# Four attention layers on one core: the order of all work written out as a literal, 274 exponentials on VectorE in place of 182

## The chip, the core and the metric

The kernel runs on one core of a Trainium2 chip. A core has five engines, each with its own instruction stream: TensorE (PE in the profile, its weight loads PEld), VectorE (DVE), ScalarE (ACT), GpSimd (POOL) and SyncE (SP), which here only issues DMAs. An engine takes its instructions in the order in which the program lists them; semaphores hold an instruction until what it needs is there. The metric is the device time of one execution in microseconds.

## The reference

Four transformer attention layers run one after the other over 2048 tokens of width 512, with weights A, B, A, B. All 32 heads share one key and one value head of width 16.

```python
q = (x @ wq).reshape(B, S, H, Dh).transpose(0, 2, 1, 3)     # H = 32, Dh = 16
k = x @ wk
v = x @ wv
scores = einsum("bhqd,bkd->bhqk", q, k) * Dh ** -0.5
p = softmax(scores)
o = einsum("bhqk,bkd->bhqd", p, v)
return o.transpose(0, 2, 1, 3).reshape(B, S, H * Dh) @ wo

x = x + A(layernorm(x));  x = x + B(layernorm(x))
x = x + A(layernorm(x));  x = x + B(layernorm(x))
```

The exponentials are the bulk of it: 4 layers x 32 heads x 2048 x 2048 of them.

## The kernel before, in words

**Tiling.** Queries are cut into 4 blocks `b` of 512, heads into 4 groups `m` of 8, keys into 16 chunks `c` of 128. A *pair* is one (layer, block, group); there are 64. A pair is worked in two halves of four heads (`odd`), and each half is a *segment*, cut further in the first pairs of each layer, whose last keys do not exist yet. There are 156 segments. A *unit* is one key chunk of one segment; there are 2048. No maximum is subtracted before the exponential; a check of the ranges at the end (`verdict`) sends the program to a second, general path if the inputs are too large, which does not run here.

**Scores.** `scores(n)` (L630 to L667) takes half a unit: two matmuls write 128 keys x 512 queries each of two heads into one PSUM tile `st` of 128 x 1024. Three such tiles exist (`NST = 3`), so TensorE can be three ahead of whoever reads them. Each of the 4096 halves is then read by one exponential.

**Exponentials.** Most are one ScalarE instruction (L660), written into a ring `pt` of 8 tiles. In a unit of the set `split` the first half goes to VectorE instead (`v_exp`, L669 to L690): a TENSOR_SCALAR (L673) reads `st` and writes an integer `e`, and six more instructions (L684, L686, L687, L688, L689, L679) turn it into the exponential with a cubic, in a tile `dpt`. The other half of the same unit goes through ScalarE into the same `dpt`. There are two `dpt` tiles, one `e` and one `mant`. The first read of `st` frees it; the other six run from SBUF.

**Weighted values.** `pv(u)` (L692 to L715) multiplies the exponentials of a whole unit with the values: four float32 matmuls (each is two records in the trace) in four column strips of the array, summed over the units of a segment into an accumulator `acc`. At a segment's end `merge` (L565 to L628) has VectorE read `acc` into `num` and `den` (two instructions, L575 or L578). After the second segment of a pair, five more instructions divide (L599 to L603, led by a RECIPROCAL) and give `ot`.

**Background work.** Everything else is made of generators that yield between pieces: queries (L434), keys and values (L391), layer norm and transposes (L349), output projections (L477), weight loads (L297). A piece is mostly three float16 matmuls that stand for one product of higher precision. A sum over several pieces is *open* from its first piece to its last. PSUM has eight banks: six are the three `st` tiles, two are called `acc0` and `acc1`. One of the two holds the running segment's sum, the other is used by the background work.

**What sets the order.** The program lists every instruction by a planner that runs while the program is built. It keeps a clock of TensorE, VectorE and ScalarE with fixed costs (L55 to L62) and, at each step, lets a short beam search (`choose`, L65 to L118, ten steps deep) say whether half a unit of scores (S), a unit of weighted values (P) or a piece of background (M) is next. VectorE's side work waits in a list `bg.low` and is let out one instruction at a time when the clock says that VectorE is free (L748). A half goes to VectorE only under the rule below; `GAP = 8` units must lie between two, and none is taken in the last six units of a segment.

```python
split_next = (nxt % 2 == 0 and n and not bg.low and clk.dve <= now + 600        # L761
              and segs[n[0]][3] - n[1] >= TAIL and nxt // 2 - state["split"] >= GAP
              and clk.exp >= now + BEHIND and ("v", l, NB - 1) in bg.done)
```

When the first P of a new segment is due, the planner finishes an open background sum first and gives the new segment the other bank:

```python
if s not in acc:                                                                # L697
    bg.close()
    clk.pe = max(clk.pe, bg.bank)
    state["idle"] = 1 - s % 2
    acc[s] = aps.tile([P, 512], F32, name="acc", tag=f"acc{s % 2}")
```

Of the kernel before, what the change touches and what calls it, by code (L numbers as in the profile page):

```python
# [19 lines left out]
P = 128  # L20
# [37 lines left out]
T_V1, T_V2, T_V3 = 1250, 750, 1250  # L58
GAP, TAIL, BEHIND = 8, 6, 0

DEPTH, WIDTH = 10, 24
P_S, P_P, P_M, P_URGENT, ACT = 266, 1000, 800, 1600, 4.0  # L62


def choose(root, price, bank):  # L65

    beam = [(0, root, 0, "")]
    for _ in range(DEPTH):
        new = {}
        for _, state, worth, work in beam:
            now, mode, exp, free, done, half, dve, room, units, is_open, steps, m_at, m_ns = state
            if room:
                at = max(now, free[0]) + CHANGE.get(mode + "S", 0) + T_S
                w = worth + P_S
                if dve:
                    e = exp  # L80
                    end = max(dve, at + LATE) + T_V1 + SYNC
                    whole = end + 2 * T_V2 + 4 * T_V3
                    lag = max(e, at + LEAD - T_S + CHANGE["MS"] - T_EXP)
                else:
                    e = lag = max(exp + T_EXP, at - T_S + LEAD)
                    end = whole = e + SYNC
                    w += ACT * T_EXP
                if not half:
                    d = done
                elif half > whole:  # L90
                    d = tuple(sorted(done + (half,)))
                else:
                    d = done + (whole,)
                n = (at, "S", e, free[1:] + (end,), d, 0 if half else whole, 0, room - 1, units, is_open,
                     steps, m_at, m_ns)
                c = at + ACT * lag - w
                if n not in new or c < new[n][0]:
                    new[n] = (c, n, w, work or "S")
            if done and (units or not is_open):
                at = max(now, done[0], 0 if units else bank) + CHANGE.get(mode + "P", 0) + T_P  # L100
                u = units - 1 if units else 99
                n = (at, "P", exp, free, done[1:], half, dve, room + 2, u, is_open, steps,
                     m_at if u else max(m_at, at + LATE + 1250 + SYNC), m_ns)
                w = worth + P_P
                c = at + ACT * max(exp, max(at, free[0]) + CHANGE["PS"] + LEAD - T_EXP) - w
                if n not in new or c < new[n][0]:
                    new[n] = (c, n, w, work or "P")
            if steps and (is_open or units >= (steps + 1) // 2):
                at = max(now, m_at) + CHANGE.get(mode + "M", 0) + m_ns
                n = (at, "M", exp, free, done, half, dve, room, units, steps > 1, steps - 1, m_at, m_ns)  # L110
                w = worth + m_ns - 3 * T_MM + price
                c = at + ACT * max(exp, max(at, free[0]) + CHANGE["MS"] + LEAD - T_EXP) - w
                if n not in new or c < new[n][0]:
                    new[n] = (c, n, w, work or "M")
        if not new:
            break
        beam = sorted(new.values(), key=lambda n: n[0])[:WIDTH]
    return beam[0][3]  # L118


class Clock:


    def __init__(self):
        self.pe = 0
        self.dve = 0
        self.mode = "M"
        self.exp = -T_EXP

    def change(self, mode):  # L130
        return CHANGE.get(self.mode + mode, 0)

    def mm(self, ns, mode="M"):
        self.pe += self.change(mode) + ns
        self.mode = mode

    def act(self):

        self.exp = max(self.exp + T_EXP, self.pe - T_S + LEAD)
        return self.exp + SYNC  # L140

    def v(self, ns):
        self.dve = max(self.dve, self.pe + LATE) + ns


class Background:
# [3 lines left out]

    def __init__(self, clk):
        self.clk = clk
        self.first = deque()
        self.low = deque()
        self.later = deque()
        self.queue = self.first
        self.done = set()
        self.open = False
        self.ready = self.bank = 0
        self.steps, self.ns = 0, 0  # L160
# [7 lines left out]
    def left(self):  # L168
        return self.first or self.later

    def at(self):
        return self.ready if self.open else max(self.ready, self.bank)

    def step(self):
        while self.left():
            if not self.open:
                self.queue = self.first or self.later
            if self.steps:
                self.clk.pe = max(self.clk.pe, self.at())
            self.steps -= 1  # L180
            try:
                self.open, self.ready, *more = next(self.queue[0])
                if not self.open:
                    self.steps, self.ns = more or (0, 0)
                return True
            except StopIteration:
                self.queue.popleft()
                self.open, self.ready, self.steps = False, self.clk.dve + SYNC, 0
                return True
        return False  # L190

    def others(self):

        while self.left() and not self.steps and self.ready <= self.clk.pe:
            self.step()

    def close(self):
        while self.open:
            self.step()

    def need(self, key):
        while key not in self.done:
            assert self.step() or self.spare(), key

    def spare(self):

        if self.low:
            ns, op = self.low.popleft()
            op()
            self.clk.dve = max(self.clk.dve, self.clk.pe) + ns  # L210
            return True
        return False
# [3 lines left out]
def fast_path(ctx, tc, x_in, weights, out, flag):  # L216
# [4 lines left out]
    xts = ctx.enter_context(tc.tile_pool(name="xts", bufs=6))  # L221
# [6 lines left out]
    ends = []  # L228
    scr = ctx.enter_context(tc.tile_pool(name="scr", bufs=1, space=DRAM))

    clk = Clock()
    bg = Background(clk)
    state = dict(idle=0, pool=None, end=False, split=-GAP, merged=0)
# [63 lines left out]
    def load_split(key, w):  # L297
# [3 lines left out]
        for c in range(NC + 2):  # L301
            if c > 1:
                t = ts[c - 2]
                V.tensor_scalar(parts[0][:, c - 2], t, WS, None, ALU.mult)
                V.scalar_tensor_tensor(parts[1][:, c - 2], t, WS, parts[0][:, c - 2],
                                       ALU.mult, ALU.subtract)
                clk.v(1100)
# [3 lines left out]
            if c:  # L311
                yield False, clk.pe + 4000
# [252 lines left out]
    def merge(s):  # L565
# [60 lines left out]
        if n < BQ:  # L626
            while bg.spare():
                pass  # L628
# [318 lines left out]
```

## Time and profile before

| what | value |
|---|---|
| time, median of 3 runs | 3728.27 us (3727.08 to 3729.49) |
| the profiled execution's own time | 3728.57 us |
| its span, first to last instruction | 3726.8 us |
| granted TensorE clock, mean | 0.995 |
| TensorE busy | 3640.9 us (98%) |
| ScalarE busy | 3613.7 us (97%), 3914 exponentials |
| VectorE busy | 2403.0 us (64%), 182 exponentials of seven instructions |
| GpSimd busy | 108.2 us (3%) |
| DMA | mean 29 GB/s |

Two engines are nearly full over the whole span and a third at two thirds. Busy time of TensorE is the time covered by matmuls from their start to a modelled end, so a matmul that is followed late can hide a short wait; how far apart matmuls start says more. ScalarE's exponentials overlap: one lasts 1076 ns by its row, and 3732 of them cover 3460.4 us, or 927 ns each.

### The profile page before, as it was taken

How to read it: one execution, taken by the hardware profiler on the slowest of the kernel's cores; microseconds unless marked ns; L12 is line 12 of the kernel's file. 1: busy time of each engine (PE TensorE's matmuls, PEld its weight loads, DVE VectorE, ACT ScalarE, POOL GpSimd, SP SyncE). 2: the span in 40 equal slices, each digit the busy share in tenths (PEclk: the TensorE clock that was granted, in tenths of full speed). 3: DMA queues.
4: the chain of work that ended last, by engine and by line, in shares of the span. 5: the costliest groups of instructions: out<-in, count | busy, mean ns of one | idle time of the engine just before them, and what ended most of it. 6: DMA issues, size and time to landing. Idle time of an engine off the chain costs nothing. (4 is left out here: it accounts for less than half of the span.)

```text
span 3726.8 us, 62299 instructions
## 1 busy us (share of the span) xinstructions
PE 3640.9 (98%) x26707; PEld 894.4 (24%) x26707; DVE 2403.0 (64%) x2962; ACT 3613.7 (97%) x3920; POOL 108.2 (3%) x122
## 2 busy tenths in 40 slices
PE   7899999999999999999999999999999999999998
PEld 2222222222222222222222222222222222222221
DVE  4576667567656766767655666666765566666665
ACT  6899999999999999999999999999999999999997
POOL 1000000000000000000000000000000000000000
PEclk9999999999999999999999999999999999999999
DMA  2110000110010000000101010000101101000000
GB/s 87 46 43 26 27 18 18 32 35 29 27 43 18 26 21 27 29 24 27 29 32 43 13 37 14 31 21 15 46 15 41 35 21 34 18 30 28 23 19 13
DMA packets 94814, 108.07 MB, mean 29 GB/s; under 512 B 15936, under 2 KB 72256, under 8 KB 94528
## 3 DMA queue, kind: packets, MB, share of 16 engines
q1 hardware_dynamic: 94208, 102.95, 8.7%
q8 instruction: 211, 3.46, 0.4%
q0 software_dynamic: 320, 1.05, 0.1%
q14 instruction: 75, 0.61, 0.1%
HBM read 70.39 MB, written 33.55 MB: 28 GB/s over the span
## 5 line engine op out<-in xcount | busy, mean ns | idle before, releaser
L660 ACT ACTIVATE pt<-st 128x1024 f32<-128x1024 f32 x3732 | 3460.4, 1076 | 67.1 <-PE st L645 66.0
L707 PE MATMUL acc<-pt,vop 128*32 128x512 f32 x14928 | 1920.1, 603 | 6.1 <-DVE qs L451 3.9
L645 PE MATMUL st<-qt,kop 64*128 64x512 f16 x8192 | 1316.5, 382 | 48.5 <-ACT pt L660 17.7
L645 PEld LDWEIGHTS <-kop 64*128 64x128 f16 x8192 | 348.2, 94 | 1727.6 <-issue 1654.2
L673 DVE TENSOR_SCALAR e<-st 128x1024 int32<-128x1024 f32 x182 | 222.9, 1225 | 775.6 <-PE st L645 775.4
L707 PEld LDWEIGHTS acc<-pt,vop 128*32 128x32 f32 x14928 | 340.8, 108 | 701.6 <-issue 670.4
L689 DVE SCALAR_TENSOR_TENSOR dpt<-dpt,mant 128x1024 f32<-128x1024 f32 x182 | 224.1, 1231 | 5.0
L679 DVE SCALAR_TENSOR_TENSOR dpt<-dpt,e 128x1024 f32<-128x1024 f32 x182 | 223.4, 1228 | 5.1
L688 DVE SCALAR_TENSOR_TENSOR dpt<-dpt,mant 128x1024 f32<-128x1024 f32 x182 | 224.1, 1232 | 3.4
L687 DVE SCALAR_TENSOR_TENSOR dpt<-mant 128x1024 f32<-128x1024 f32 x182 | 222.0, 1220 | 0.0
L599 DVE RECIPROCAL den<-den 128x512 f32<-128x512 f32 (+1 forms) x76 | 215.9, 2841 | 0.3
L660 ACT ACTIVATE dpt<-st 128x1024 f32<-128x1024 f32 x182 | 192.1, 1055 | 4.1 <-ACT pt L660 3.7
L707 PE MATMUL acc<-dpt,vop 128*32 128x512 f32 x1456 | 192.5, 601 | 0.0
L491 DVE SCALAR_TENSOR_TENSOR xt<-ops,xt 128x512 f32<-128x512 f32 x140 | 96.2, 687 | 146.0 <-PE ops L336 144.9
L684 DVE TENSOR_SCALAR mant<-e 128x1024 int32<-128x1024 int32 x182 | 129.0, 709 | 4.5
L686 DVE TENSOR_SCALAR e<-e 128x1024 int32<-128x1024 int32 x182 | 127.4, 700 | 5.3
L455 POOL TENSOR_TENSOR sq<-qs 128x512 bf16<-128x512 f16 x64 | 66.7, 1042 | 2119.1 <-DVE qs L450 2119.1
L578 DVE SCALAR_TENSOR_TENSOR num<-acc,half,num 128x512 f32<-128x512 f32 x92 | 68.9, 749 | 86.9 <-PE acc L707 86.6
L334 PE MATMUL qps<-xnT,wq 128*128 128x512 f16 x256 | 99.6, 389 | 0.7 <-ACT xnT L330 0.7
L335 PE MATMUL qps<-xnT,wq 128*128 128x512 f16 x256 | 98.0, 383 | 0.2 <-DVE xnT L384 0.2
L450 DVE TENSOR_SCALAR qs<-qps 128x512 f16<-128x512 f32 x64 | 43.9, 687 | 83.5 <-PE qps L336 72.7
L334 PE MATMUL ops<-wo,ot 128*128 128x512 f16 x252 | 97.6, 387 | 0.0
(99 smaller groups left out, 1413.3 us busy)
## 6 DMA issues: line engine op xcount, KB each, us to landing
qt<-qs SPq DMA_DIRECT2D x624, 64.0 KB, 2.2
qs<-qs SPq DMA_DIRECT2D x64, 256.0 KB, 2.2
xs<-xt SPq DMA_DIRECT2D x48, 256.0 KB, 2.0
xt<-xs SPq DMA_DIRECT2D x48, 256.0 KB, 3.2
xt<-in_A_x_dram SPq DMA_DIRECT2D x32, 256.0 KB, 3.4
out_dram<-xt SPq DMA_DIRECT2D x16, 256.0 KB, 2.0
wst<-in_A_wo_dram SPq DMA_DIRECT2D x8, 256.0 KB, 2.8
wst<-in_B_wq_dram SPq DMA_DIRECT2D x8, 256.0 KB, 2.8
```

What stands on the lines that cost most here:

```text
L334: PE.matmul(ps, a[0], b[0], start=first, stop=False)
L599: (6 * n, lambda c=c: V.reciprocal(den[:, c], den[:, c])),
L645: PE.matmul(st[:, k * 512:(k + 1) * 512], kop[l % 2][c // 4][r, (c % 4) * P:(c % 4 + 1) * P], qt[pr][r, 2 * half + odd], start=True, stop= ...
L660: e = nc.scalar.activation(pt, st, AF.Exp, scale=SCALE / UP / UP).ins
L673: V.tensor_scalar(e, st, SCALE / UP / UP * LOG2E * 2.0 ** 23, 127 * 2.0 ** 23, ALU.mult, ALU.add)
L679: V.scalar_tensor_tensor(p, p, C0, e.bitcast(F32), ALU.add, ALU.mult)
L684: (T_V2, lambda: V.tensor_scalar(mant.bitcast(I32), e, 0x7FFFFF, 0x3F800000, ALU.bitwise_and, ALU.bitwise_or)),
L686: (T_V2, lambda: V.tensor_scalar(e, e, 0x7F800000, None, ALU.bitwise_and)),
L687: (T_V3, lambda: V.scalar_tensor_tensor(p, mant, C3, mant, ALU.add, ALU.mult)),
L688: (T_V3, lambda: V.scalar_tensor_tensor(p, p, C2, mant, ALU.add, ALU.mult)),
L689: (T_V3, lambda: V.scalar_tensor_tensor(p, p, C1, mant, ALU.add, ALU.mult)),
L707: PE.matmul(acc[s][32 * j:32 * j + 32, :], v[l % 2][c // 4][:, c % 4, 16 * odd:16 * odd + 32], p_of[u, j % 2][:, (j // 2) * 512:(j // 2 + ...
```

## The change: what it does

The planner, its clock and its cost table are gone. In their place stands a string `ORDER` of 8972 letters that is walked once while the program is built. `S` is half a unit of scores with its exponential on ScalarE, `V` the same with the exponential on VectorE; `v` is the next of the six instructions that follow on VectorE; `P` and `Q` are the first or second waiting unit of weighted values; `M` and `m` are a piece of background, `l` one from the list of less urgent ones; `d` is the next instruction of a division. The string has 3822 S, 274 V, 1644 v, 2048 P and Q, 804 pieces of background and 380 d.

The instructions themselves keep their form and shape. Beside the order, these things differ:

- 92 more halves go to VectorE, and as many fewer to ScalarE.
- A background sum may stay open when a new segment begins. Then the new segment's accumulator takes the bank of the segment that has just ended, which `merge` must have read by then.
- `xts`, the pool of rows of `x`, has 8 buffers, not 6.

```diff
-T_MM, T_S, T_P, T_TR, T_EXP, LEAD, SYNC, LATE = 216, 226, 860, 490, 917, 1449, 55, 270
-CHANGE = {"SP": 89, "PS": 139, "SM": 97, "PM": 149, "MS": 96, "MP": 93}
...
-def choose(root, price, bank):
...
+ORDER = (
+    "mSSSMMMSSSPPSSMSSPPSSMMSSSPPSSMMSSPSSPPSSSPPSSMMSSSMMSPSSPSSMPSmSPSSPPSSSPmPSMSSPSSPPSSSMPSPSSSPMSSPSSPM"
+    "SSPSmSMMSSPSMMSSPSSPSSMPSmSPPSSSPPSSPmSSPMSSPSSMSPSSPPSMSSSPPSSSPMSSPSmSMMMSSSMPSSPSSPPSMSSPmSSPPSSSPPmS"
...
-    xts = ctx.enter_context(tc.tile_pool(name="xts", bufs=6))
+    xts = ctx.enter_context(tc.tile_pool(name="xts", bufs=8))
...
-    def scores(n):
+    def scores(n, on_v):
...
+        if on_v:
+            split.add(u)
...
+        if half:
+            waiting.append(u)
+        if on_v:
+            v_exp(pt, st)
             return
...
-    def pv(u):
+    def pv(k):
+
+        u = [u for u in waiting if u[0] == state["seg"]][k]
+        waiting.remove(u)
...
         if s not in acc:
-            bg.close()
-            clk.pe = max(clk.pe, bg.bank)
-            bg.bank = state["merged"]
-            state["idle"] = 1 - s % 2
-            acc[s] = aps.tile([P, 512], F32, name="acc", tag=f"acc{s % 2}")
+
+            if not bg.open:
+                state["idle"] = 1 - state["idle"]
+            acc[s] = aps.tile([P, 512], F32, name="acc", tag=f"acc{1 - state['idle']}")
             left[s] = c1 - c0
...
+        nxt = 0
+        for what in ORDER:
+            if what in "SV":
+                scores(nxt, what == "V")
+                nxt += 1
+            elif what in "PQRT":
+                pv("PQRT".index(what))
+            elif what in "Mml":
+                bg.step(what == "l")
             else:
...
+                (exp_ops if what == "v" else div_ops).popleft()()
+        assert nxt == 2 * len(units) and not waiting and not div_ops
```

How the instructions move is seen best on VectorE. Below is VectorE's list in the kernel before, from the end of the 75th segment (in layer 1), whose `acc` it reads into `num` and `den`; `e<-st` is the first instruction of a VectorE exponential, `dpt<-dpt,e` its last, and the numbers behind names count allocations.

```order
L575 TENSOR_SCALAR num_14447<-acc,half 128x512
L575 TENSOR_SCALAR den_14448<-acc,half 128x512
L688 SCALAR_TENSOR_TENSOR dpt<-dpt,mant 128x1024
L689 SCALAR_TENSOR_TENSOR dpt<-dpt,mant 128x1024
L679 SCALAR_TENSOR_TENSOR dpt<-dpt,e_14393 128x1024
L673 TENSOR_SCALAR e_14514<-st 128x1024
L684 TENSOR_SCALAR mant<-e_14514 128x1024
L686 TENSOR_SCALAR e_14514<-e_14514 128x1024
L687 SCALAR_TENSOR_TENSOR dpt<-mant 128x1024
L450 TENSOR_SCALAR qs<-qps 128x512
L451 TENSOR_TENSOR qs<-qps,qs 128x512
```

The change has this at the same place:

```order
L515 TENSOR_SCALAR num_14761<-acc,half 128x512
L515 TENSOR_SCALAR den_14762<-acc,half 128x512
L611 TENSOR_SCALAR mant<-e_14750 128x1024
L613 TENSOR_SCALAR e_14750<-e_14750 128x1024
L614 SCALAR_TENSOR_TENSOR dpt<-mant 128x1024
L615 SCALAR_TENSOR_TENSOR dpt<-dpt,mant 128x1024
L436 SCALAR_TENSOR_TENSOR xt<-ops,xt 128x512
L616 SCALAR_TENSOR_TENSOR dpt<-dpt,mant 128x1024
L617 SCALAR_TENSOR_TENSOR dpt<-dpt,e_14750 128x1024
L609 TENSOR_SCALAR e_14844<-st 128x1024
```

From this segment's end to the end of the second segment after it, the list before starts three exponentials and the list of the change four. Over the whole program two starts lie 16 halves apart at the least before, and mostly 10 to 16 halves apart in the change.

On TensorE, the kernel before has this where the 75th segment gives way to the 76th; `vop_3` and `vop_0` tell the two apart, since the first is multiplied with the last chunks' values and the second with the first ones':

```order
L645 MATMUL st<-qt,kop_0_101 128x512
L707 MATMUL acc<-pt,vop_3_112 32x512 x4
L707 MATMUL acc<-pt,vop_0_109 32x512 x4
L645 LDWEIGHTS kop_1_102
L645 MATMUL st<-qt,kop_1_102 128x512
```

The change has this there:

```order
L636 MATMUL acc<-dpt,vop_3_112 32x512
L581 LDWEIGHTS kop_0_101
...
L297 LDWEIGHTS ot_0_13556
L297 MATMUL ops<-wo_9598,ot_0_13556 128x512
L298 LDWEIGHTS ot_0_13556
L298 MATMUL ops<-wo_9599,ot_0_13556 128x512
L299 LDWEIGHTS ot_1_13557
L299 MATMUL ops<-wo_9598,ot_1_13557 128x512
L581 LDWEIGHTS kop_1_102
...
L636 MATMUL acc<-pt,vop_0_109 32x512 x8
```

Two halves of scores, the first piece of an output projection (`ops`, left open) and two more halves have come between the segments, and two units of weighted values now follow each other. Since the sum of `ops` stays open in the other bank, the 76th segment's sum goes where the 75th's was. That happens at 33 of the 155 segments' starts after the first.

More of the change, by code (lines that the diff above doesn't have):

```diff
@@ L51 @@
 LOG2E = 1.4426950408889634
-T_MM, T_S, T_P, T_TR, T_EXP, LEAD, SYNC, LATE = 216, 226, 860, 490, 917, 1449, 55, 270
-CHANGE = {"SP": 89, "PS": 139, "SM": 97, "PM": 149, "MS": 96, "MP": 93}
[L58 to L62, printed above, removed]
-def choose(root, price, bank):
[L71 to L118, printed above, removed]
@@ L121 @@
-class Clock:
-    def __init__(self):
[L125 to L143, printed above, removed]
@@ L153, in __init__ @@
+class Background:
+    def __init__(self):
         self.first = deque()
-        self.low = deque()
         self.later = deque()
@@ L166, in add_later, with step @@
         self.later.extend(gens)
[L168 to L199, printed above, removed]
-    def need(self, key):
[L202 to L212, printed above, removed]
+    def step(self, later=False):
+        if not self.begun:
+            self.queue = self.later if later or not self.first else self.first
+        self.begun = True
+        try:
+            self.open = next(self.queue[0])
+        except StopIteration:
+            self.queue.popleft()
+            self.open = self.begun = False
+    def need(self, key):
+        assert key in self.done, key
 @with_exitstack
@@ L227, in fast_path @@
     exps = []
-    ends = []
     scr = ctx.enter_context(tc.tile_pool(name="scr", bufs=1, space=DRAM))
-    clk = Clock()
-    bg = Background(clk)
-    state = dict(idle=0, pool=None, end=False, split=-GAP, merged=0)
+    bg = Background()
+    state = dict(idle=0, pool=None, end=False, seg=0)
+    exp_ops = deque()
+    div_ops = deque()
     def bank(name):
@@ L515, in verdict @@
     def verdict():
-        yield False, clk.pe, 1, T_MM
+        yield False
         n, nv = NL * NB, NL * NB + 8
@@ L560, in fast_path @@
     left = {}
-    ring = {}
-    done = {}
+    waiting = []
     split = set()
@@ L623, in then @@
                         bg.add_later(load_split(("wq", l + 2), weights[l % 2][0]))
-        bg.low.append((0, then))
-        if n < BQ:
-            while bg.spare():
-                pass
-    def scores(n):
+        op = div_ops.pop()
+        div_ops.append(lambda: (op(), then()))
+    def scores(n, on_v):
         u, half = units[n // 2], n % 2
@@ L654, in scores @@
             pt = pts[:, len(exps) % NPT]
-            ring.setdefault(u, len(exps))
         p_of[u, half] = pt
-        if u in split and half == 0:
-            v_exp(u, pt, st)
+        if half:
+            waiting.append(u)
+        if on_v:
+            v_exp(pt, st)
             return
@@ L665, in scores, with v_exp @@
             exps.append(e)
-        ends.append(clk.act())
-        done[u] = max(done.get(u, 0), ends[-1])
-    def v_exp(u, p, st):
+    def v_exp(p, st):
         e = one.tile([P, W * 512], I32, name="e2")
@@ L788, in fast_path @@
-        while bg.spare():
-            pass
+        nxt = 0
[7 more added lines that the diff above has]
+                bg.step(what == "l")
+            else:
+                (exp_ops if what == "v" else div_ops).popleft()()
+        assert nxt == 2 * len(units) and not waiting and not div_ops
         state["end"] = True
-        while bg.step():
-            pass
+        while bg.first or bg.later:
+            bg.step()
```

230 lines of the change are left out of this document (118 added, 112 removed).

## The prediction, made blind

> **What bounds the kernel now.** I read the page's busy times first, then the groups of instructions, then stretches of time, then who waits for whom, and last TensorE's timeline.
>
> ```profile
> span 3726.8 us, 62299 instructions
> PE 3640.9 (98%) x26707; PEld 894.4 (24%) x26707; DVE 2403.0 (64%) x2962; ACT 3613.7 (97%) x3920; POOL 108.2 (3%) x122
> L660 ACT ACTIVATE pt<-st 128x1024 f32<-128x1024 f32 x3732 | 3460.4, 1076 | 67.1 <-PE st L645 66.0
> L660 ACT ACTIVATE dpt<-st 128x1024 f32<-128x1024 f32 x182 | 192.1, 1055 | 4.1 <-ACT pt L660 3.7
> L707 PE MATMUL acc<-dpt,vop 128*32 128x512 f32 x1456 | 192.5, 601 | 0.0
> ```
>
> TensorE and ScalarE are both full, and the profiled execution took 3728.57 us, 0.3 above the median of the runs. The stretches show that this is so all the way, not as an average of two kinds of stage:
>
> ```profile
> 900.00:1800.00 900.00, 893.71 (x6598) 220.13 (x6591) 598.46 (x725) 890.62 (x967) 24.86 (x23) 1.00 0.09 28
> 1800.00:2700.00 900.00, 891.86 (x6581) 217.97 (x6579) 576.28 (x694) 890.83 (x968) 23.93 (x23) 1.00 0.08 27
> ```
>
> Columns: the stretch, then TensorE, weight loads, VectorE, ScalarE and GpSimd with their counts. ScalarE does 967 instructions in 890.62 us, 0.921 us each, and idles 9.4 of 900 us. Relieving it alone helps only as far as TensorE has room, so the question is how much of TensorE's 98% is work. Its timeline in the middle:
>
> ```profile
> 1499.71 1.07 PE L707 MATMUL acc<-pt,vop 128*32 128x512 f32 x8
> 1500.70 0.61 PE L645 MATMUL st<-qt,kop 64*128 64x512 f16 x4
> 1501.25 1.92 PE L707 MATMUL acc<-pt,vop 128*32 128x512 f32 x16
> 1503.11 0.61 PE L645 MATMUL st<-qt,kop 64*128 64x512 f16 x4
> 1503.64 1.06 PE L707 MATMUL acc<-pt,vop 128*32 128x512 f32 x8
> 1504.64 0.61 PE L645 MATMUL st<-qt,kop 64*128 64x512 f16 x4
> 1505.18 0.39 PE L334 MATMUL ops<-wo,ot 128*128 128x512 f16 x1
> 1505.40 0.38 PE L335 MATMUL ops<-wo,ot 128*128 128x512 f16 x1
> ...
> 1506.27 0.38 PE L336 MATMUL ops<-wo,ot 128*128 128x512 f16 x1
> 1506.58 0.61 PE L645 MATMUL st<-qt,kop 64*128 64x512 f16 x4
> ...
> 1509.64 0.39 PE L645 MATMUL st<-qt,kop 64*128 64x512 f16 x2
> 1509.96 1.07 PE L707 MATMUL acc<-pt,vop 128*32 128x512 f32 x8
> ```
>
> I read the distances from start to start. A half of scores (x2) before a P takes 0.32 us (1509.64 to 1509.96). Two halves before a P take 0.55 (1500.70 to 1501.25), so a half before a half takes 0.23. A P (x8) before scores takes 0.99 (1499.71 to 1500.70), two take 1.86 (1501.25 to 1503.11), so a P before a P takes 0.87. A background matmul takes 0.22 before its like and 0.31 before scores (1506.27 to 1506.58), and a half before background 0.54 - 0.23 = 0.31. So each change of kind has a price: S to P 0.09, P to S 0.12, M to S 0.09, S to M 0.08. For the rare M to P and P to M, which are not in this piece, I take 0.09 and 0.12 as for the same kind left or entered.
>
> With these, TensorE's floor. The built order before has 4096 halves, 2048 P and 2131 background matmuls, and of changes 1481 S to P, 1540 P to S, 398 M to S, 457 S to M, 102 M to P and 43 P to M. Work: 4096 x 0.23 + 2048 x 0.87 + 2131 x 0.22 = 942 + 1782 + 469 = 3193 us. Changes: 133 + 185 + 36 + 37 + 9 + 5 = 405 us. The floor is 3598 us. The first score starts late and the program ends long after the last P:
>
> ```profile
> 33.69 0.58 PE L645 MATMUL st<-qt,kop 64*128 64x512 f16 x1 [7.29 <-DMA qt<-qs]
> 3701.32 0.70 PE L645 MATMUL st<-qt,kop 64*128 64x512 f16 x4
> 3704.34 2.95 PE L707 MATMUL acc<-pt,vop 128*32 128x512 f32 x24
> ```
>
> From 33.7 to 3726.8 are 3693 us, some 95 to 105 over the floor, and about 18 of them lie behind the last P (3707 to 3726.8, with little matmul in it). The row at 3701.32 shows what the rest looks like: two halves that cover 0.70 us, not the 0.61 seen above. A wait of under 0.2 us hides inside TensorE's busy time, because a matmul's modelled end is later than the next one's earliest start. The waits that do show:
>
> ```profile
> PE st L645 <- ACT pt L660: 17.7, 48, 0.5
> PE st L645 <- DVE kop L415: 5.5, 3, 2.6
> PE st L334 <- DVE ot L602: 5.4, 3, 3.4
> PE acc L707 <- DVE qs L451: 3.9, 4, 1.6
> ACT pt L660 <- PE st L645: 66.0, 59, 10.6
> ```
>
> Columns: who waits for whom, total us, times, longest. So of the 100 us, 18 are the tail, some 12 to 15 are waits for VectorE and DMA, and up to 70 are waits for a free `st` tile, that is for ScalarE: 17.7 visible, the rest hidden. ScalarE in turn has 66 us of waits for TensorE, 10.6 of them at the start. Two engines of equal load (ScalarE 3914 x 0.921 = 3605 us, TensorE 3598) lean on each other through three buffers, and both lose.
>
> **The change part by part.**
>
> *Fewer changes of kind on TensorE.* The order of the change has the same matmuls, with 1401 S to P, 1388 P to S, 446 M to S, 433 S to M, 25 M to P and 38 P to M: 290 changes fewer. -80 x 0.09 - 152 x 0.12 + 48 x 0.09 - 24 x 0.08 - 77 x 0.09 - 5 x 0.12 = -7.2 - 18.2 + 4.3 - 1.9 - 6.9 - 0.6 = **-30 us**, all on the path, since TensorE bounds. The new floor is 3568 us.
>
> *92 halves from ScalarE to VectorE.* At 3460.4 / 3732 = 0.927 us this takes 85 us from ScalarE: 3822 x 0.921 = 3520 us are left, 48 under TensorE's new floor where the two were level. It shortens the path only through the waits for `st`. At most it takes all 70 us; nothing, if these come from the latency of a buffer's round and not from ScalarE's pace. I take **-40**, a little over half: 48 us of lead in 3568 is 1.3%, some 0.01 us per half, so a backlog drains only slowly.
>
> *What that costs VectorE.* The seven instructions of an exponential:
>
> ```profile
> L673 DVE TENSOR_SCALAR e<-st 128x1024 int32<-128x1024 f32 x182 | 222.9, 1225 | 775.6 <-PE st L645 775.4
> L684 DVE TENSOR_SCALAR mant<-e 128x1024 int32<-128x1024 int32 x182 | 129.0, 709 | 4.5
> L686 DVE TENSOR_SCALAR e<-e 128x1024 int32<-128x1024 int32 x182 | 127.4, 700 | 5.3
> L687 DVE SCALAR_TENSOR_TENSOR dpt<-mant 128x1024 f32<-128x1024 f32 x182 | 222.0, 1220 | 0.0
> L679 DVE SCALAR_TENSOR_TENSOR dpt<-dpt,e 128x1024 f32<-128x1024 f32 x182 | 223.4, 1228 | 5.1
> L578 DVE SCALAR_TENSOR_TENSOR num<-acc,half,num 128x512 f32<-128x512 f32 x92 | 68.9, 749 | 86.9 <-PE acc L707 86.6
> ```
>
> With L688 and L689 of the same form as L679, one is 1.225 + 0.709 + 0.700 + 1.220 + 3 x 1.228 = 7.54 us, and 92 are 694 us. VectorE goes from 2403 to 3097 us, 85% of some 3660. It hides beside TensorE and ScalarE as long as each chain ends before its P is due. Laid end to end with the distances above, TensorE has a median of 12.3 us of work between a VectorE half and its P (13.8 before), and VectorE lists 9.6 us from the chain's first to its last instruction, others in between included (9.6 before). The room is 3.4 us in the median and 1.2 us at the tenth part of the chains (4.2 and 2.1 before). Start, handing over and any backlog come out of that. For the tight tenth, 27 chains, up to 1 us each could show: 0 to +27 us. Today no P waits for a chain (0.0 before the `dpt` matmuls, above).
>
> *Sums left open over a segment's end.* At 33 starts the new sum waits until VectorE has read the old one: 2 x 0.749 = 1.5 us. Between the old sum's last P and the new one's first, the order lists at least two halves, three background matmuls and two halves: 0.23 + 0.31 + 2 x 0.22 + 0.31 + 0.23 + 0.32 = 1.84 us behind the last P's 0.99, or 1.96 behind the 0.87 that a P lasts; half of the places have 2.6 or more. So nothing shows, unless VectorE is busy with one more instruction of 1.23 us: then the 13 places with 1.96 wait 0.8 us each and some others 0.1, 0 to +12 us. For both VectorE terms I take **+5**, near the low end, since the row nearest to them is the 0.0.
>
> *At nothing:* the two further `xts` buffers (no row of the waits names the loads of `x`), and the same DMAs in another order (the queues are used 9%). The start and the 18 us tail stay.
>
> Sum: 3728.6 - 30 - 40 + 5 = **3663 us**, 1.7% less.
>
> [...]
>
> **The rivals.**
>
> *ScalarE alone is the bound.* TensorE's stretched distances would close up as soon as ScalarE is faster, and all 85 us come through: 3728.6 - 85 = 3643. For it: ScalarE's 9 us idle in 900. Against it: the piece of timeline above, in which TensorE has no gap. [...]
>
> *The waits for `st` stay.* They come from the round of three buffers (matmul, handing over, exponential, handing back) and not from ScalarE's load. Then only the changes of kind count: 3728.6 - 30 = 3699. For it: the 48 visible waits are at most 0.5 us long, so no backlog stands behind them.
>
> *VectorE late, the slower side.* VectorE works strictly in its listed order. An instruction at its head that waits for TensorE holds the rest of a chain behind it, and the P waits for that. Today it stands idle ahead of its exponentials for 775.4 us in 182 chains, and has 3727 - 2403 = 1324 us idle in all; then it has some 566. Each 0.1 us by which a chain is late on average costs 27 us; the saving of 70 us is gone at 0.26 us per chain. With 0.4 us it is 3728.6 - 70 + 110 = 3769. Against it: 3.4 us of room in the median. [...]
>
> *It hardly does what it says.* The order moves 92 halves and 290 changes, so no effect could only come from gains and losses that cancel: 3728.
>
> **How the numbers follow.** The forecast has 0.50, ScalarE alone 0.20, the waits that stay 0.17, VectorE late 0.09, no effect 0.04. Differences under 0.2% cannot be told from none in this kernel. Faster is the sum of the first three, 0.87; same 0.04; slower 0.09. The best case, all of the 70 and no loss, is 3728.6 - 100 = 3629; the range's other end takes in the rival with 3699 and 13 us of its VectorE terms: 3628 to 3712.
>
> **What would show it.** ScalarE's exponentials at x3548 and x274 and its idle time up by some 20 us, with waits for TensorE ahead of them; TensorE's wait for `pt` under 17.7 us; distances unchanged at 0.23, 0.87 and 0.99; VectorE at about 3097 us. The forecast fails if the `dpt` matmuls or the first `acc` of a segment show tens of us of idle time (VectorE late), if the changes of kind cost otherwise than by one piece of timeline, or if TensorE's floor was no floor: a span under 3602, the new floor of 3568 and the start of 34.

## The result

The change takes 3644.07 us (median of 4 runs, 3641.05 to 3644.58) where the kernel before takes 3728.3: a ratio of 0.9772, 95% interval 0.9755 to 0.9789, or 84 us less. The forecast was 3663, with 3628 to 3712 as its range. The profiled execution took 3641.05 us, its span is 3639.3 us. One of the four executions of a later run, the one with 273 VectorE halves, took 11958.87 us at a granted TensorE clock of 0.28; what is said of that run is from the other three.

Below are the profile page's and the stretches' lines of the kernel after, with the same columns as the lines of before.

```profile
span 3639.3 us, 63025 instructions
PE 3575.5 (98%) x26707; PEld 925.5 (25%) x26707; DVE 3084.4 (85%) x3606; ACT 3552.5 (98%) x3828; POOL 116.8 (3%) x122
L598 ACT ACTIVATE pt<-st 128x1024 f32<-128x1024 f32 x3548 | 3311.5, 1046 | 41.0 <-PE st L581 30.4
L636 PE MATMUL acc<-dpt,vop 128*32 128x512 f32 x2192 | 290.8, 602 | 0.0
L609 DVE TENSOR_SCALAR e<-st 128x1024 int32<-128x1024 f32 x274 | 335.3, 1224 | 199.3 <-PE st L581 194.8
...
900.00:1800.00 900.00, 896.97 (x6742) 233.61 (x6738) 762.96 (x881) 893.70 (x964) 29.52 (x25) 1.00 0.09 28
1800.00:2700.00 900.00, 896.59 (x6739) 234.78 (x6735) 764.59 (x886) 892.84 (x962) 29.58 (x25) 1.00 0.09 29
```

VectorE does 274 exponentials and is busy for 3084 us, as worked out (3097). No P waits for a VectorE chain: 0.0 ahead of the `dpt` matmuls. In the same 900 us TensorE now runs 6742 matmuls instead of 6598, 2.2% more, and its idle time there falls from 6.3 to 3.0 us. ScalarE does not idle more, as I had expected, but less: 3639 - 3553 = 87 us in all instead of 113.

The waits of the kernel after:

```profile
PE st L581 <- ACT pt L598: 8.1, 28, 0.5
PE st L581 <- DVE kop L369: 5.9, 4, 2.6
PE st L297 <- DVE ot L540: 4.7, 3, 3.4
PE st L581 <- DVE e L609: 0.5, 1, 0.5
...
ACT pt L598 <- PE st L581: 30.4, 42, 11.2
```

TensorE's visible wait for ScalarE fell from 17.7 to 8.1 us, ScalarE's for TensorE from 66.0 to 30.4. Both sides wait less. The waits that hide in busy time are seen in the distances from start to start, taken here from all matmuls of both traces by what stands ahead and what behind (S a half of scores, P a unit of weighted values, M a background matmul); "beyond" is the sum of what each distance lies over the usual one of its class.

```
            before                         after
        count  usual ns  beyond us     count  usual ns  beyond us
S to S   2158    227      114.8         2262    227       67.4
S to P   1481    319        6.3         1401    310        8.9
P to S   1540    998        3.8         1388    998        4.3
P to P    465    882        2.0          622    883        0.0
S to M    457    312        3.6          433    312        7.9
M to S    398    312       12.6          446    312       12.6
all 9    8274              167.8        8274             120.2
sum of all distances: 3705.6 us before, 3618.6 us after
```

The 87 us between the two sums are 30 for other counts at the usual distances, 47 for shorter waits between two halves of scores, and 10 spread thinly over the rest. (Ahead of a P the usual distance shrank by 9 ns, but the mean by under 3, which is 4 us.)

The traces also say who keeps a half waiting. A half needs the tile of the half three before it, and nearly every half that starts late (over 0.02 us beyond its usual distance) starts 0.04 to 0.06 us after the read of that tile has ended. Put to these readers, the late halves are ScalarE's: 106.8 us (649 halves) before and 63.8 us (516) in the change. VectorE's reads hold 4.6 us before and 0.5 us in the change. So far this is the forecast's picture, waits for tiles that ScalarE has not yet read, with the term larger. Whether the lighter ScalarE or the new order brings the 47 is for the experiments to say.

### The profile page after: what moved, and what is told of

The parts are those of the page before. It is cut to its first block, busy times and chain, and to the rows that moved or that the text cites. A ratio compares the mean times of both kernels' runs of the same rounds, so it can differ in the third digit from the quotient of the medians.

```text
span 3639.3 us, 63025 instructions
## 1 busy us (share of the span) xinstructions
PE 3575.5 (98%) x26707; PEld 925.5 (25%) x26707; DVE 3084.4 (85%) x3606; ACT 3552.5 (98%) x3828; POOL 116.8 (3%) x122
## 4 chain that ended last, share of the span: by engine, by line
PE 86%; ACT 11%; DVE 2%; DMA 1%; issue 0%; SPq 0%; POOL 0%; ACTq 0%; DVEq 0%; POOLq 0%
PE acc L636 47%; PE st L581 27%; ACT pt L598 10%; PE qps L297 2%; PE ops L297 2%; PE qps L298 1%; PE qps L299 1%; PE ops L299 1%; PE ops L298 1%; ACT dpt L598 1%; PE tps L338 1%; PE kps L297 0%; DVE den L537 0%; PE kps L299 0%; PE kps L298 0%
## 5 line engine op out<-in xcount | busy, mean ns | idle before, releaser
L598 ACT ACTIVATE pt<-st 128x1024 f32<-128x1024 f32 x3548 | 3311.5, 1046 | 41.0 <-PE st L581 30.4
L636 PE MATMUL acc<-pt,vop 128*32 128x512 f32 x14192 | 1799.5, 601 | 0.1
L609 DVE TENSOR_SCALAR e<-st 128x1024 int32<-128x1024 f32 x274 | 335.3, 1224 | 199.3 <-PE st L581 194.8
L617 DVE SCALAR_TENSOR_TENSOR dpt<-dpt,e 128x1024 f32<-128x1024 f32 x274 | 339.7, 1240 | 8.5
L615 DVE SCALAR_TENSOR_TENSOR dpt<-dpt,mant 128x1024 f32<-128x1024 f32 x274 | 338.9, 1237 | 7.1
L616 DVE SCALAR_TENSOR_TENSOR dpt<-dpt,mant 128x1024 f32<-128x1024 f32 x274 | 336.9, 1230 | 7.6
L614 DVE SCALAR_TENSOR_TENSOR dpt<-mant 128x1024 f32<-128x1024 f32 x274 | 336.4, 1228 | 0.0
L636 PE MATMUL acc<-dpt,vop 128*32 128x512 f32 x2192 | 290.8, 602 | 0.0
L598 ACT ACTIVATE dpt<-st 128x1024 f32<-128x1024 f32 x274 | 282.9, 1033 | 5.0 <-ACT pt L598 4.3
L613 DVE TENSOR_SCALAR e<-e 128x1024 int32<-128x1024 int32 x274 | 193.6, 707 | 7.9
L297 PE MATMUL qps<-xnT,wq 128*128 128x512 f16 x256 | 99.1, 387 | 1.4 <-DVE wq L269 0.7
L298 PE MATMUL qps<-xnT,wq 128*128 128x512 f16 x256 | 97.4, 380 | 0.6 <-DVE xnT L342 0.6
L299 PE MATMUL qps<-xnT,wq 128*128 128x512 f16 x256 | 97.3, 380 | 0.4 <-DVE wq L270 0.4
```

Of the source, the lines that this page charges most:

```text
L297: PE.matmul(ps, a[0], b[0], start=first, stop=False)
L598: e = nc.scalar.activation(pt, st, AF.Exp, scale=SCALE / UP / UP).ins
L609: V.tensor_scalar(e, st, SCALE / UP / UP * LOG2E * 2.0 ** 23, 127 * 2.0 ** 23, ALU.mult, ALU.add)
L613: lambda: V.tensor_scalar(e, e, 0x7F800000, None, ALU.bitwise_and),
L614: lambda: V.scalar_tensor_tensor(p, mant, C3, mant, ALU.add, ALU.mult),
L615: lambda: V.scalar_tensor_tensor(p, p, C2, mant, ALU.add, ALU.mult),
```

## The experiments

Three theories went into them. A, the forecast: TensorE's work and its changes of kind are the floor, and ScalarE adds waits for a free `st` tile. B: ScalarE alone is the bound, and the time follows its load. C: VectorE's lateness limits (first as the fixed round of the three tiles, C, then as C', the chains themselves).

### ScalarE's load halved, in both orders

```diff
-        e = nc.scalar.activation(pt, st, AF.Exp, scale=SCALE / UP / UP).ins
+        if u in split:
+            e = nc.scalar.activation(pt, st, AF.Exp, scale=SCALE / UP / UP).ins
+        else:
+            e = nc.scalar.activation(pt[:, :512], st[:, :512], AF.Exp, scale=SCALE / UP / UP).ins
...
+    V.memset(pts[:, :, 512:], 1.0)
     with tc.manual_schedule():
```

On the order of the change:

> The changed kernel, in which each ScalarE exponential of a unit that lies on ScalarE alone covers 512 of the 1024 columns; the other 512 columns of the ring are set to one at the start, so half of these exponentials are not computed. The order is untouched. It takes ScalarE from the path and shows TensorE's floor in this order. Theory A: 3568 + 34 (start) + 18 (tail) + some 13 (waits for VectorE and DMA) = 3633 us, so only 5 to 20 us less than the change: 3624 to 3639 us. Theory B: TensorE has room, and the time falls by 100 us or more. Theory C: the waits for score tiles shrink because the round of a tile is shorter by 0.43 us: like A.

On the order before:

> The kernel before with the same halving of ScalarE's exponentials (512 of 1024 columns for units on ScalarE alone, half of these not computed), order untouched. It shows TensorE's floor in the order before. Theory A: 3598 + 34 + 18 + 13 = 3663 us, 30 us above the same edit of the change. Theory B: the same time as the same edit of the change, far below 3600 us. Theory C: like A.

The change with half the exponentials of `pt` took 3579.55 us, the kernel before with the same edit 3640.66 us. The pages' busy lines, first of the change's order, then of the order before:

```profile
PE 3519.8 (98%) x26707; PEld 835.7 (23%) x26707; DVE 3082.9 (86%) x3607; ACT 2185.6 (61%) x3828; POOL 117.2 (3%) x122
```

```profile
PE 3569.8 (98%) x26707; PEld 811.4 (22%) x26707; DVE 2403.1 (66%) x2963; ACT 2203.5 (61%) x3920; POOL 108.8 (3%) x122
```

ScalarE is at 61% in both, and TensorE stays at 98%. This settles the main point against B: with some 1400 us of ScalarE's busy time gone, the change is only 65 us faster, the kernel before only 88. With ScalarE lightened so far, TensorE's listed order sets the time, and it is 61 us shorter in the change. It also shows that the forecast's floor was too high: 3602 us with the start was named as what would refute it, and the span is 3577.8. By the distances of the two halved runs, 30 of the 61 us are again the other counts and 23 are waits between two halves (35.1 us beyond the usual before, 11.8 in the change), although ScalarE holds no tile long in either. What holds them is mostly VectorE's first read. Its visible waits, the first line from the order before, the second from the change's:

```profile
PE st L645 <- DVE e L676: 9.9, 19, 0.9
```

```profile
PE st L581 <- DVE e L612: 4.1, 11, 0.6
```

VectorE has 92 exponentials more in the second and yet TensorE waits less for tiles that VectorE is to read. Put to their readers as above, hidden waits included, the late halves held by VectorE are 27 us in the order before and 9 in the change; ScalarE holds 4 and 2. VectorE is not late in the order before: all its 182 reads start 0.42 to 0.46 us after the half's second matmul. What differs is TensorE's own list. A VectorE half's tile is free some 1.7 us after the half has started. In the order before, 86 of the 182 VectorE halves have less than that, at the usual distances, between them and the third half behind; all 86 of these third halves wait, 25 us in all. In the literal order none of the 274 has less than 1.76 us there.

### ScalarE's load alone, taken off and put on

Every 20th exponential halved in the order before:

```diff
-        e = nc.scalar.activation(pt, st, AF.Exp, scale=SCALE / UP / UP).ins
+        state["acts"] = state.get("acts", 0) + 1
+        w = 512 if u not in split and state["acts"] % 20 == 10 and len(exps) >= NPT else W * 512
+        e = nc.scalar.activation(pt[:, :w], st[:, :w], AF.Exp, scale=SCALE / UP / UP).ins
```

> The kernel before, order untouched, in which every 20th ScalarE exponential (of units on ScalarE alone) covers 512 of its 1024 columns, so that these are half left out. Some 186 times 0.43 us = 80 us less work for ScalarE, about what the change takes from it (85), with nothing else moved. It measures what ScalarE's relief is worth alone. Theory A (in the order before, TensorE at 3641 without ScalarE's load): a part of the 88 us between 3641 and 3728, in proportion to the load taken away (halving all took away some 1600 us) or, since the waits arise only where ScalarE is behind, up to 30 us: 3698 to 3720 us. Theory B: 80 us: 3648 us.

It took 3718.21 us, 10 less than before (ratio 0.9973, 0.9963 to 0.9983). The groups of this run show the relief and where it went:

```profile
L662 ACT ACTIVATE pt<-st 128x1024 f32<-128x1024 f32 x3543 | 3326.3, 1057 | 108.6 <-PE st L645 104.7
L662 ACT ACTIVATE pt<-st 128x512 f32<-128x512 f32 x189 | 121.2, 642 | 2.5 <-PE st L645 2.5
```

189 exponentials last 642 instead of 1057 ns, 78 us less in all. ScalarE's idle time ahead of its exponentials went from 67.1 to 111.1 us: in an order that is left as it was, a lighter ScalarE mostly waits for TensorE. The halves held by ScalarE's reads went only from 107 to 97 us. B's 80 us are refuted here, and ScalarE's lead alone, from which the forecast got its second term, does not bring that term in this order.

The other way round, copies added on ScalarE in the order of the change:

```diff
         e = nc.scalar.activation(pt, st, AF.Exp, scale=SCALE / UP / UP).ins
+        state["acts"] = state.get("acts", 0) + 1
+        if state["acts"] % 24 == 20:
+            if state["acts"] == 20:
+                state["x"] = one.tile([P, 512], F16, name="spare")
+                V.memset(state["x"], 1.0)
+            nc.scalar.copy(state["x"], state["x"])
```

> The changed kernel with 159 copies of 512 columns within SBUF added on ScalarE, one after every 24 exponentials, order otherwise untouched. At some 0.5 to 0.6 us each that is 80 to 95 us more work for ScalarE, as much as the change took from it. Theory A: TensorE's order has room of its own only at places, so a part comes through, 25 to 50 us: 3670 to 3694 us. Theory B: all of it: 3724 to 3739 us.

It took 3714.48 us, 70 more than the change. Its group of copies, and TensorE's longest wait:

```profile
L604 ACT COPY spare<-spare 128x512 f16<-128x512 f16 x159 | 101.3, 637 | 0.0
```

```profile
PE st L581 <- ACT pt L598: 44.2, 132, 1.0
```

The load was 101 us, a little more than planned, and about 70% of it came through; the halves held by ScalarE's reads rose from 64 to 130 us. The run before this one took work off and this one puts it on, but in different orders, so that 70% come through here and an eighth there can lie in the direction or in the order.

Side by side they bound what the lighter ScalarE and the new order are worth alone. The old order with a lighter ScalarE takes 3718 us, 10 less than before. The new order with 101 us put on ScalarE takes 3714, 14 less; at 70%, the 85 us that the change took off would make it some 3703, 25 less, which is an estimate. Both together bring 84. So most of the 84 us comes from the two together and from neither alone. The added load and the relief do not stand where the 92 halves stood, so these are bounds and not exact shares.

### The VectorE halves, fewer and more

49 of the 274 halves given back to ScalarE in the literal order; the edit is in the string: V becomes S at 49 places, their 294 v are left out, and where the ring of `pt` asks for it the unit's P is taken in listed order. The first place:

```diff
...
-PvSSQvQSVSQvSSvSPvPvSSSvQQvSMSVSQmSSSPPSSSQvQmSvSSvM
+PvSSQvQSSSQSSSPPSSSQPSMSVSPmSSSPPSSSQvQmSvSSvM
...
```

> The changed kernel with 49 of its 274 VectorE halves given back to ScalarE (their six following instructions are left out, and the units' weighted values come in listed order where the exponential ring asks for it); the changes of kind on TensorE stay as they are in the change. Theory A (TensorE's work and changes of kind are the floor, ScalarE adds only waits for a free score tile): of the 84 us that the change saved, 30 are the changes of kind, 54 the waits; 49 of 92 halves give back 49/92 x 54 = 29 us: 3673 us. Theory B (ScalarE alone is the bound): 49 x 0.927 = 45 us: 3689 us. Theory C (the waits for score tiles do not depend on ScalarE's load, only the order counts): no change, 3644 us.

3684.08 us, 40 more: between A's 29 and B's 45, nearer to B. ScalarE's wait for TensorE hardly rose, from 30.4 to 33.4 us, but TensorE's for ScalarE went from 8.1 to 27.2:

```profile
PE st L578 <- ACT pt L595: 27.2, 67, 0.5
```

Hidden waits included, the halves held by ScalarE's reads rose from 64 to 105 us, which is all of the 40. In the literal order ScalarE's load is what these waits depend on. Of the 49 halves 31 lie in the last layer, and the places of some P moved with them.

273 halves under the planner of before, with its rule loosened:

```diff
-GAP, TAIL, BEHIND = 8, 6, 0
+GAP, TAIL, BEHIND = 4, 4, -2000
...
-            split_next = (nxt % 2 == 0 and n and not bg.low and clk.dve <= now + 600
+            split_next = (nxt % 2 == 0 and n and not state.get("late") and len(bg.low) <= 5 and clk.dve <= now + 3000
```

> The kernel before, with its planner, whose rule for giving a half to VectorE is loosened (at least 4 units apart, none in the last 4 units of a segment, allowed while ScalarE is up to 2 us ahead and VectorE up to 3 us behind with 5 pieces of side work left). It gives 273 halves to VectorE, and the planner's own list of S, P and M has 68 changes of kind fewer than before (3941, not 4009; the literal order has 3919). Theory A: 68 x 0.105 = 7 us for the changes, up to 54 for the waits: 3667 us if VectorE's chains come in time. Theory B: 91 x 0.927 = 84 us: 3644 us. Theory C: 3721 us. If VectorE's chains come late (the planner does not lay them out ahead): above 3700 us, with idle time ahead of the matmuls that read a VectorE exponential.

3810.0 us, 82 more than before (ratio 1.0221, 1.0200 to 1.0241). Its waits:

```profile
PE st L645 <- ACT pt L660: 29.2, 81, 0.6
PE acc L707 <- DVE dpt L679: 28.1, 10, 4.8
...
PE st L645 <- DVE e L673: 15.0, 25, 1.5
```

```profile
ACT pt L660 <- PE st L645: 149.3, 129, 10.6
```

This is the forecast's slower rival: P waits for a chain up to 4.8 us, and ScalarE's waits more than double. Part of the 82 us is TensorE's clock. Seven of the ten waits of P for a chain, 2.1 to 4.8 us long, go with a stretch of 3.4 to 10.2 us at a granted clock of 0.50, 44 us in all, so up to 22 us are lost to the slower clock, an estimate that takes half of the 44 (the mean granted clock is 0.990 in this run, 0.995 before); in one of them two P lie 1.70 us apart (854.02 to 855.72), not 0.88. The kernel before has such stretches only in its first 183 us and in its tail. The count of VectorE halves is within one of the change's. Their number brings nothing by itself; the order that is laid around them decides the sign.

17 more halves, put by hand into the literal order at the starts of the layers, where VectorE has the most idle time (in the change it is busy for 31 of the 60 us from 120 us on and for 21 of the 60 from 960 us on); the first of them:

```diff
...
-SSPMSSPSSPMSSPSmSMMSSPSMMSSPSSPSSMPSmSPPSSSPP
+SSPMSSPSVPMvSSvPvSmSvMMvSSQvSMMSSQSSQSSMPSmSPPSSSPP
...
```

> The changed kernel with 17 more halves on VectorE (291), put where its order has few, at the start of the layers; each one's six further instructions are spread over the 12 us after it, and its P comes so much later in the segment. 16 us less for ScalarE, 128 us more for VectorE (88% of the time). Theory A: a part of ScalarE's relief, up to 10 us less, if the chains come in time: 3634 to 3644 us. If VectorE's instructions collide with the reads of background sums there: 5 to 30 us more.

3688.55 us, 44 more than the change. I had not expected more than 30. ScalarE's wait for TensorE went from 30.4 to 82.6 us:

```profile
PE st L582 <- DVE kop L370: 9.6, 4, 4.5
PE st L582 <- ACT pt L599: 8.8, 30, 0.5
PE ops L298 <- DVE xt L437: 7.9, 6, 2.8
```

The visible waits for the keys (`kop`, 5.9 before) and for the reads of the output projections (`xt`, 3.7 before) grew by 8 us; both stand behind added instructions in VectorE's list. Another 21 us are in the distances from a P to the half behind it (25.5 us beyond the usual, 4.3 in the change). They lie inside the P: 46 P go on more than 0.15 us late after they have begun, 31 us in all (16 P and 4 us in the change), and 28 of the 46 go on within 0.15 us of the end of a ScalarE instruction. So many of them have begun with one of their unit's exponentials and wait for ScalarE's other. Of the 44 us, then, some 27 lie inside P, and some 8 are seen to be VectorE's list at a layer's start.

### VectorE slower

```diff
-            lambda: V.scalar_tensor_tensor(p, mant, C3, mant, ALU.add, ALU.mult),
+            lambda: [V.scalar_tensor_tensor(p, mant, C3, mant, ALU.add, ALU.mult) for _ in range(2)],
```

> The changed kernel in which each of the 274 VectorE exponentials does its third instruction (the first step of the cubic) twice: 1.23 us more per chain, 337 us more in all, VectorE from 3084 to 3421 us (94% of 3640). It doubles the suspected cost of the change. Theory A (the chains have 3.4 us of room in the median, 1.2 at the tenth part): the tight tenth shows, 27 x 0.6 us, and some backlog: +20 to +60 us. Theory C' (VectorE late is what already limits the change): most of the 337 us come through, +200 us or more.

3782.83 us, 139 more than the change: 0.51 us of each 1.23 comes through. A said 20 to 60, C' 200 and more; neither holds. The waits tell where:

```profile
PE st L581 <- DVE e L609: 79.7, 136, 1.8
PE acc L636 <- DVE dpt L617: 21.9, 27, 2.1
```

Most of it is not a P that waits for its chain, as the forecast had it. It is TensorE waiting for the `st` tile that VectorE has not yet read, since the read stands behind other VectorE work: in 102 of the 136 waits the read begins some 0.1 us behind the last instruction of the chain ahead of it, in the others behind a division or other side work. The reads start 1.12 us after the half's second matmul in the median, 0.43 in the change. Hidden waits included, VectorE's reads hold 107 us of halves, 0.5 in the change. There are 27 waits of P for a chain, as many as the forecast called tight; the 136 of the first line it had not thought of. VectorE keeps to its list: in the trace of the change all 2298 instructions of its chains and divisions start in the order of the string's V, v and d.

### Changes of kind, more and fewer

In the string, 145 places SSPP become SPSP; the first of them:

```diff
...
-SSSMMMSSSPPSSMSSPPSSMMSSSPPSSMM
+SSSMMMSSPSPSSMSPSPSSMMSSPSPSSMM
...
```

> The changed kernel with 145 places SSPP in its order turned into SPSP, spread over the program: the first P comes one half of scores earlier, the second half one P later. That is 290 changes of kind more, as many as the change took away; VectorE's and ScalarE's work is the same. Theory A (changes of kind lie on the path at the prices of the distances): 145 x (0.09 + 0.12) = +30 us, 3674 us. Theory B (ScalarE alone bounds): no change, 3644 us, but up to 145 x 0.4 us more if ScalarE is left without scores by the later half.

3669.29 us, 25 more: 25 / 290 = 0.087 us per change, against the forecast's 0.105 from one piece of timeline. TensorE's wait for ScalarE stayed at 8.1 us, and ScalarE's for TensorE rose from 30.4 to 44.9, so what is paid is TensorE's own time:

```profile
ACT pt L598 <- PE st L581: 44.9, 100, 10.6
```

33 places SPSP become SSPP; the first:

```diff
...
-SVPvSmSSPSPvSSvSmQSQvSQvSSmSQv
+SVPvSmSSSPPvSSvSmQSSQvQvSSmSQv
...
```

> The changed kernel with 33 places SPSP turned into SSPP: 66 changes of kind fewer. Theory A: 66 x 0.087 (the price of the run with 290 more) = 6 us less, 3638 us, less what the later P and the earlier half wait. Theory B: no change.

3646.41 us (3645.55 to 3646.65), 2 more rather than 6 less. Its waits show why:

```profile
PE st L581 <- ACT pt L598: 17.1, 43, 0.6
```

Bringing the half forward makes it wait for its tile: 17.1 us for ScalarE, not 8.1. The price of a change is real when one is added, and these 33 could not be taken away for nothing in this way.

### Sums closed at a segment's end

```diff
-            if not bg.open:
-                state["idle"] = 1 - state["idle"]
+            while bg.open:
+                bg.step()
+                state["ahead"] = state.get("ahead", 0) + 1
+            state["idle"] = 1 - state["idle"]
...
+            elif what in "Mm" and state.get("ahead", 0):
+                state["ahead"] -= 1
             elif what in "Mml":
```

> The changed kernel in which an open background sum is finished before a new segment's first P, as in the kernel before, and the new sum goes to the bank that the background sum has just left; the pieces that come early are left out where the order lists them later. VectorE's and ScalarE's work is the same, and TensorE has 52 changes of kind fewer (3679, not 3731). Theory A: -5 us for the changes, but at 33 places the first P waits until VectorE has read the background sum that ended right ahead of it, 0.3 + 0.69 us, and 1.2 us more if VectorE is in a longer instruction: +33 to +70 us; 3670 to 3710 us. If the open sums are worth nothing: 3640 us.

> The same as the run with the sums closed, and ScalarE's exponentials of units on ScalarE alone cover 512 of 1024 columns (half of these left out), as in the two halved runs, which stand at 3580 us (order of the change) and 3641 us (order before). 25 of these 61 us are the changes of kind at the price that the run with 290 more gave. Theory A: open sums are what is left of the difference, some 30 us: 3605 to 3615 us. If they are worth nothing: 3575 us, and the rest is where VectorE's work was put.

3724.74 us, 81 more than the change; with ScalarE halved 3642.66 us, 63 more than the same without the edit. Both lie above what either theory named. The first run's waits:

```profile
PE acc L638 <- DVE qs L401: 42.5, 26, 2.0
PE st L581 <- ACT pt L598: 34.0, 76, 0.7
```

At 31 segment starts the first P now stands right behind a background matmul, 1.2 to 2.4 us after its start and mostly over 1.8, not 0.31. That is the wait for a bank, 51 us in all by the distances. The rest goes with it: scores listed behind that P come later, ScalarE's wait for TensorE went from 30.4 to 108.4 us, and the halves held by ScalarE's reads from 64 to 101.

I would not read 81 us as what the open sums brought. In the kernel before, the planner kept background work away from these places: 152 of its 155 segment starts have nothing between the last P and the first but halves of scores, and the first P waits there 8 us in all. The literal order puts background matmuls there 33 times. It can do so only with open sums, but how much of the 61 us that its order is shorter comes from this freedom cannot be had by closing them in an order laid for open ones.

## Why the prediction was right, and where it was off

**The sum.** 3728.6 - 30 - 40 + 5 = 3663 against 3644, 19 us too high. Term by term, by the distances of the two traces:

- *Fewer changes of kind, -30.* The counts at the usual distances give 30. Put on by experiment, 290 changes cost 25. This step held.
- *Waits for `st`, -40.* The waits between two halves fell by 47, and they are mostly waits for ScalarE's reads of `st`, as forecast (106.8 us of them before, 63.8 in the change). That 40 came near 47 is partly luck: it was a little over half of 70, and the waits to take it from were 115. What the step "it shortens the path only through the waits for `st`" left out is that ScalarE's lead of 48 us does not do this alone. Taking 78 us of load off in the order before brought 10 us, and putting load back in the literal order cost 40 and 70. What the 92 halves bring depends on how the scores, P and VectorE's reads are laid around them: a planned order with 273 VectorE halves is 82 us slower than before, the literal one with 274 is 84 us faster.
- *The rest, -10.* The forecast had no term for it: the other distances shrank by some 10 us on balance, no kind of them by as much as 4 us.
- *VectorE, +5.* No P waits for a chain and 0.5 us is waited for a VectorE read of `st`: 0 to 1 us. Of the 33 starts with an open sum 12, not 13, have the shortest list of work, and none of the 33 waits over 0.15 us.
- *The floor, 3598 and 3568.* Too high. The halved run of the change has a span of 3577.8 us with its start, tail and waits. Two steps were mis-sized: 0.22 us per background matmul, where the trace has 0.206 from one background matmul to the next (280 of the 1630 start under 0.2 us apart in the trace of before), some 30 us; and the 34 us of the start and the 18 of the tail were added to a floor that already holds the 56 background matmuls in them, some 12 us. So the waits in the kernel before were not 70 us at most but 115 between halves alone.

**The sign and the rivals.** "ScalarE alone is the bound" came nearest in its time (3643 for 3644) and is refuted in its mechanism: halving ScalarE's exponentials brings 65 us where it needed 100 or more, taking 78 us off ScalarE alone brings 10 where it needed 80, and 30 of the 84 us are TensorE's changes of kind. What is right in it: in the literal order, load added to ScalarE cost about 70% of itself as copies and 40 of 45 us as exponentials. "The waits for `st` stay" fell with the 47 us. "VectorE late" did not occur in the change, but it occurs in the planner's order with 273 halves and with one more instruction per chain.

**What the profile was to show.** x3548 and x274, VectorE near 3097, the distances at 227, 882 and 998 ns and TensorE's wait for `pt` under 17.7 us all came. ScalarE's idle time was to rise by 20 us and fell by 26. The span is some 22 us shorter than forecast, and ScalarE is busy for 3553 us instead of the 3520 worked out: its exponentials cover 3311.5 / 3548 = 0.933 us each, not 0.927 or 0.921.

**What stays open.** The 61 us by which the literal order is shorter with ScalarE halved are 30 for changes of kind and 23 for waits between halves, most of these behind VectorE reads that the list before leaves too little time for. With ScalarE's full load the waits between halves are mostly for ScalarE's reads. There, the share of the lighter ScalarE and that of the order are only bounded, by the runs with load taken off and put on. What the open sums bring was not isolated.

## What to carry to other kernels

When two engines are level and a third is at two thirds, read the distances from start to start before believing a busy share of 98% (before the change the distances show 115 us of waits between halves, the visible waits for ScalarE 17.7), and price every change of kind from them. Here, moving work from one full engine to a freer one paid only with an order that was laid anew around it: nearly the same number of moved pieces gave 84 us less in one order and 82 us more in another, and the new order with 101 us put back on ScalarE kept only 14 of the 84. When a tile is held, ask who reads it and how much listed work stands ahead of its next writer. An engine with idle time was not free for more work here: VectorE was busy for 85% of the time and kept to its list, and what others waited for then stood behind the added instructions. 17 more halves on it cost 44 us. One instruction more in each of 274 chains cost 139 us, with 79.7 us of visible waiting for its first read of the shared tile `st` and 21.9 for the ends of the chains.

## What the runs showed of the hardware that I had not expected

- ScalarE's load counts unevenly: 101 us added to it in the change's order cost 70, 78 us taken away in the order before brought 10; direction and order are not separated.
- In the planner's order with 273 halves, seven waits of TensorE of 2.1 to 4.8 us go with stretches of 3.4 to 10.2 us at a granted clock of 0.50.
- A VectorE instruction of 1.23 us added to each of 274 chains cost 0.51 us each, three quarters of the visible waiting for it at the PSUM tile (79.7 us) and not at the consumer of the chain (21.9 us).
- A change of kind on TensorE between a half of scores (`64*128` in the rows) and a P (`128*32`) cost 0.087 us each when 290 were added.
